# Sliding-window attention with scores made twice in 32-row tiles, so that probabilities come out transposed

## The chip, the cores and the metric

The kernel runs on one core of a Trainium2 chip. The time is that of one execution on the device, in microseconds, as the median of several; executions of one kernel mostly agree within about 1% here. Runs are compared only with runs of the kernel before that were taken on the same chip in the same rounds. In the views, PE is TensorE (PEld its weight loads, which overlap), DVE is VectorE, ACT is ScalarE, POOL is GpSimd. PEclk, the granted clock, is the share of full speed that the throttle let TensorE have. Tiles named `..._ps` take TensorE's results and lie in PSUM; one buffer of such tiles is called a bank here. A matmul shown as `32*128 32x128` uses 32 rows and 128 columns of the array and moves 128 columns through it; a tiling mode is the size of the part of the array that a matmul addresses.

## The reference

Two branches over the same `x` (2048 x 640, bfloat16) are mixed by a gate. The change concerns the first one, attention over a window of 256 keys with 32 heads of 20 columns:

```python
def _A_ref(x, wqkv, wo):                      # S = 2048, D = 640, H = 32, Dh = 20, W = 256
    q, k, v = ...                             # (x @ wqkv), split into heads
    scores = einsum('bhqd,bhkd->bhqk', q, k) * Dh ** (-0.5)
    mask = (idx[:, None] - idx[None, :] >= 0) & (idx[:, None] - idx[None, :] < W)
    p = softmax(where(mask, scores, -1e9))
    o = einsum('bhqk,bhkd->bhqd', p, v)
    return o.transpose(...).reshape(B, S, D) @ wo
# b = _B_ref(...): a recurrence over 64 segments of 32 with 8 memory rows, 32 heads of 192
g = sigmoid((x * gate_w).sum(-1, keepdims=True))
return g * _A_ref(x, ...) + (1 - g) * b
```

## The kernel before

Four parts run one after the other: the sliding branch (`branch_A`), projections for the tails of all segments (`tail_projections`), the recurrent branch (`branch_B`) and the mix. In the sliding branch a head has only 20 of the 128 rows that a full matmul contracts over (`128*128` in the views). Q and K of four heads share 128 rows, 32 each. To get one head's scores, Q is kept in four copies (`QTm`), each zero outside one head's rows; the matmul then runs over all 128 rows. The masks are added by two more matmuls, DVE finds the maximum, ACT takes the exponential, and PE transposes the probabilities for the product with V.

```python
# branch_A: P = 128, KT = 5 (640 / 128), NB = 16 query blocks, NG = 8 groups of 4 heads, NKB = 3 key blocks
ps_s = ctx.enter_context(tc.tile_pool(name="a_ps_s", bufs=5, space=bass.MemoryType.PSUM))
ps_t = ctx.enter_context(tc.tile_pool(name="a_ps_t", bufs=2, space=bass.MemoryType.PSUM))
ps_o = ctx.enter_context(tc.tile_pool(name="a_ps_o", bufs=1, space=bass.MemoryType.PSUM))
# [...] weights: Wq and Wk padded to 32 columns a head (WqP, WkP); m_first, m_last: 0 or -1e30
QTm = [[const.tile([P, NG, P], BF, name=f"QTm{b}_{r}") for r in range(4)] for b in range(2)]
for b in range(2):
    for r in range(4):
        (nc.vector if (b + r) % 2 == 0 else nc.gpsimd).memset(QTm[b][r][:], 0.0)
# [...] prep_units(qb) returns closures: load and transpose x, gate, and:
    def mk_qk(isq, g0):
        def u():
            xT = stt['xT']
            Wp = WqP if isq else WkP
            ng = min(4, NG - g0)
            pst = ps_s.tile([P, 512], FP32, name="qk_ps", tag="s")
            for gg in range(ng):
                g = g0 + gg
                for kt in range(KT):
                    nc.tensor.matmul(pst[:, gg * P:(gg + 1) * P],
                                     lhsT=Wp[:, kt, 4 * g:4 * g + 4, :].rearrange("p h d -> p (h d)"),
                                     rhs=xT[:, kt, :], start=(kt == 0), stop=(kt == KT - 1))
            src = pst[:, 0:ng * P].rearrange("p (g q) -> p g q", q=P)
            if isq:
                nc.scalar.mul(stt['QT'][:, g0:g0 + ng, :], src, scale)
                for r in range(4):
                    nc.gpsimd.tensor_copy(qms[qb][r][32 * r:32 * r + DH, g0:g0 + ng, :],
                                          stt['QT'][32 * r:32 * r + DH, g0:g0 + ng, :])
            else:
                nc.vector.tensor_copy(stt['KTb'][:, g0:g0 + ng, :], src)
                if g0 + ng >= NG:
                    kring[qb] = stt['KTb']
        return u
# [...] mk_v: V of the block, with a column of ones
# for each query block qb, with nxt = prep_units(qb + 1), qm = qms[qb], kbs = its 2 or 3 key blocks:
    def st_scores(h):
        g, r = h // 4, h % 4
        sp = ps_s.tile([P, 512], FP32, name="s_ps", tag="s")
        for ci, c in enumerate(kbs):
            need_mask = (c == qb) or (c == qb - (NKB - 1))
            nc.tensor.matmul(sp[:, ci * P:(ci + 1) * P], lhsT=qm[r][:, g, :], rhs=kring[c][:, g, :],
                             start=True, stop=not need_mask)
            if need_mask:
                nc.tensor.matmul(sp[:, ci * P:(ci + 1) * P], lhsT=ident[:],
                                 rhs=(m_last if c == qb else m_first)[:], start=False, stop=True)
        nmx = hp.tile([P, 1], FP32, name="a_nmx")
        nc.vector.tensor_reduce(out=nmx[:], in_=sp[:, 0:nk * P], axis=AX.X, op=ALU.max, negate=True)
        ex = hp.tile([P, NKB * P], BF, name="a_ex")
        nc.scalar.activation(out=ex[:, 0:nk * P], in_=sp[:, 0:nk * P], func=ACT.Exp, bias=nmx[:], scale=1.0)
        hs[h] = dict(ex=ex)

    def st_transpose(h):
        if h % 2 == 0:
            return
        pt_ps = ps_t.tile([P, 2, NKB, P], BF, name="pt_ps", tag="t")
        for a in range(2):
            ex = hs[h - 1 + a]['ex']
            for ci in range(nk):
                nc.tensor.transpose(pt_ps[:, a, ci, :], ex[:, ci * P:(ci + 1) * P], ident[:])
        pt = hp.tile([P, 2, NKB, P], BF, name="a_pt", bufs=4)
        if h % 4 == 1:
            nc.scalar.copy(pt[:, :, 0:nk, :], pt_ps[:, :, 0:nk, :])
        else:
            nc.vector.tensor_copy(pt[:, :, 0:nk, :], pt_ps[:, :, 0:nk, :])
        for a in range(2):
            hs[h - 1 + a]['pt'] = pt[:, a]

    def st_pv(h):
        pt = hs[h]['pt']
        half = h // HH
        if h % HH == 0:
            o_tiles[half] = ps_o.tile([P, HH, 32], FP32, name="o_ps", tag="o")
        ovh = o_tiles[half]
        for ci, c in enumerate(kbs):
            nc.tensor.matmul(ovh[:, h % HH, 0:DH + 1], lhsT=pt[:, ci, :], rhs=vring[c][:, h, :],
                             start=(ci == 0), stop=(ci == nk - 1))
        del hs[h]
        if h % HH == HH - 1:
            rl = op.tile([P, HH], FP32, name="rl")
            nc.vector.reciprocal(rl[:], ovh[:, :, DH:DH + 1].rearrange("p h o -> p (h o)"))
            nc.vector.tensor_tensor(out=an[:, half * HH:(half + 1) * HH, :], in0=ovh[:, :, 0:DH],
                                    in1=rl[:].unsqueeze(2).to_broadcast([P, HH, DH]), op=ALU.mult)
    nu = len(nxt)
    every = max(1, (HA - 4) // max(1, nu))
    ui = 0
    for i in range(HA + 6):
        if i < HA:
            st_scores(i)
        if 0 <= i - 3 < HA:
            st_transpose(i - 3)
        if 0 <= i - 5 < HA and i % 2 == 0:
            st_pv(i - 6)
            st_pv(i - 5)
        if ui < nu and i >= 2 and (i - 2) % every == 0:
            nxt[ui](); ui += 1
    while ui < nu:
        nxt[ui](); ui += 1
# [...] transposes of `an`, output projection (10 matmuls), gate, store
# the whole kernel
early, late, last = weights.resident[:34], weights.resident[34:-2], weights.resident[-2:]
# early: loaded while branch_A runs; late: issued after it, ahead of tail_projections; last: ahead of branch_B
branch_A(...); tail_projections(...); branch_B(...); mix_out(...)
```

## Time and profile before

| | us |
|---|---|
| time before, median of the first 3 runs | 2617.16 |
| sliding branch in the profiled run, up to the tail's first matmul | 526.9 |
| tail projections, up to the first recurrent matmul | 185.8 |
| recurrent branch and mix | 1887.3 |

The prediction below shows the stages, a block's groups and the waits. Two more views matter for what follows. The first is the head of the page of the kernel before: busy time by engine, then PE's busy share and the granted clock in 40 slices of the span, in tenths.

```profile
PE 2249.0 (86%) x49877; PEld 1664.5 (64%) x49893; DVE 1190.4 (46%) x3578; ACT 1115.8 (43%) x2433; POOL 601.9 (23%) x1782
...
PE   7888889889888888888898888889888888889885
...
PEclk9899998989999899999999999999998999999987
```

The second is 100 us in the middle of the sliding branch. The columns are stretch, length, busy time (and instructions) of PE, PEld, DVE, ACT and POOL, granted clock, DMA share, GB/s.

```profile
200.00:300.00 100.00, 88.41 (x1405) 74.51 (x1410) 72.94 (x161) 73.00 (x139) 22.16 (x50) 0.92 0.07 20
```

The sliding branch is the first eight slices. PE is busy for seven to nine tenths of each, and its clock there is about as high as elsewhere: 0.92 in this stretch. Busy time does not say at which clock it was spent, so the two lines are read together.

### The profile page before, as it was taken

The numbers are of one execution on the slowest core, as the hardware profiler recorded it, in microseconds if no ns is written. First come the engines' busy times: TensorE is split into PE (matmuls) and PEld (weight loads), VectorE is DVE, ScalarE is ACT, GpSimd is POOL, SyncE is SP. The second block draws the span as 40 slices with busy tenths as digits, with TensorE's granted clock in tenths as the row PEclk, the third lists the DMA queues.
The fourth block names the chain that finished last, engine by engine and source line by source line (L and its number), as shares of the span: only waits on it lengthen the run. The fifth ranks groups of instructions, "written<-read, shape, count | busy, mean of one in ns | idle before, by whom it ended". The sixth has DMA issues, their size and how long they took to land.

```text
span 2600.0 us, 113795 instructions
## 1 busy us (share of the span) xinstructions
PE 2249.0 (86%) x49877; PEld 1664.5 (64%) x49893; DVE 1190.4 (46%) x3578; ACT 1115.8 (43%) x2433; POOL 601.9 (23%) x1782
## 2 busy tenths in 40 slices
PE   7888889889888888888898888889888888889885
PEld 5777777679465666666666656666666566566663
DVE  5777777723233443444344334434443444334433
ACT  4777777712233333333333333333333333333333
POOL 7622222050122222222222222222222221222220
PEclk9899998989999899999999999999998999999987
DMA  6600000085588888888888888888888888888887
GB/s 211 204 17 17 17 17 15 9 253 154 143 273 264 268 284 278 281 278 291 289 274 282 290 268 271 290 287 283 281 282 272 279 270 271 280 285 278 286 274 235
DMA packets 299154, 591.76 MB, mean 228 GB/s; under 512 B 102552, under 2 KB 112032, under 8 KB 298656
## 3 DMA queue, kind: packets, MB, share of 16 engines
q1 hardware_dynamic: 275536, 525.43, 62.9%
q0 software_dynamic: 20160, 55.60, 6.5%
q8 instruction: 391, 6.41, 1.0%
q10 hardware_dynamic: 2960, 3.44, 0.4%
q14 instruction: 107, 0.88, 0.1%
HBM read 554.98 MB, written 36.97 MB: 228 GB/s over the span
## 4 chain that ended last, share of the span: by engine, by line
PE 52%; DMA 34%; ACT 10%; DVE 2%; issue 2%; SPq 0%; POOL 0%; ACTq 0%; DVEq 0%; POOLq 0%
DMA t_w<-w_packed 30%; PE ps_o L764 8%; PE ps_q L599 8%; PE ps_k L599 8%; PE ps_v L599 5%; ACT a_ex L195 4%; PE t_psum L440 3%; ACT a_pt L208 3%; PE qk_ps L124 3%; PE ps_pv L740 2%; PE tr_k L614 2%; PE S_ps L668 2%; PE t_psv L457 1%; PE pt_ps L205 1%; PE S_ps L661 1%
## 5 line engine op out<-in xcount | busy, mean ns | idle before, releaser
L599 PEld LDWEIGHTS <-t_hT 128*32 128x32 bf16 x15360 | 379.6, 98 | 302.5 <-issue 93.2
L764 PE MATMUL ps_o<-t_OT,w_o 128*128 128x40 bf16 x8960 | 333.2, 182 | 41.7 <-ACT t_OT L745 41.7
L764 PE MATMUL ps_o<-t_OT,t_w 128*128 128x40 bf16 x6400 | 269.5, 182 | 111.5 <-DMA t_w<-w_packed 99.9
L764 PEld LDWEIGHTS <-w_o 128*128 128x128 bf16 x8960 | 288.0, 98 | 49.0 <-issue 42.9
L764 PEld LDWEIGHTS <-t_w 128*128 128x128 bf16 x6400 | 209.6, 97 | 140.6 <-DMA t_w<-w_packed 136.7
L745 ACT CAST t_OT<-ps_pv 128x480 bf16<-128x480 f32 x256 | 143.2, 559 | 327.5 <-PE ps_pv L740 327.2
L195 ACT ACTIVATE a_ex<-s_ps,a_nmx 128x384 bf16<-128x384 f32 (+2 forms) x512 | 252.8, 576 | 65.9 <-DVE a_nmx L193 63.7
L646 POOL COPY t_K<-t_xqk 128x64 bf16<-128x64 bf16 x256 | 60.8, 237 | 936.5 <-PE S_ps L668 656.3
L193 DVE TENSOR_REDUCE a_nmx<-s_ps 128x1 f32<-128x384 f32 (+2 forms) x512 | 247.0, 524 | 33.7 <-PE s_ps L190 25.1
L604 ACT CAST t_tok<-ps_k 128x384 bf16<-128x384 f32 x256 | 122.7, 479 | 314.1 <-PE ps_k L599 314.1
L723 DVE TENSOR_TENSOR t_PTx<-PT_ps,mk_x 128x320 bf16<-128x320 f32 x256 | 125.2, 489 | 266.8 <-PE PT_ps L716 266.8
L599 PE MATMUL ps_q<-w_q,t_hT 128*32 128x384 bf16 x4096 | 225.9, 343 | 18.7 <-DVE t_hT L775 18.4
L599 PE MATMUL ps_v<-w_v,t_hT 128*32 128x384 bf16 x4352 | 230.1, 335 | 0.0
L599 PE MATMUL ps_k<-w_k,t_hT 128*32 128x384 bf16 x4096 | 222.4, 338 | 0.0
L637 DVE COPY t_K<-tr_k 128x256 bf16<-128x256 bf16 x256 | 74.0, 289 | 244.1 <-PE tr_k L614 242.8
L604 ACT CAST t_tok<-ps_q 128x384 bf16<-128x384 f32 x256 | 123.0, 481 | 129.7 <-PE ps_q L599 129.5
L187 PE MATMUL s_ps<-KT_blk,QTm 128*128 128x128 bf16 x1440 | 172.5, 225 | 4.5 <-ACT a_ex L195 4.0
L604 ACT CAST t_vtok<-ps_v 128x384 bf16<-128x384 f32 x256 | 122.7, 479 | 116.6 <-PE ps_v L599 115.2
L614 PEld LDWEIGHTS <-t_tok 128*128 128x128 bf16 x1536 | 87.6, 98 | 117.4 <-ACT t_tok L604 56.4
L775 DVE CAST t_hT<-ps_o 128x40 bf16<-128x40 f32 x63 | 12.6, 200 | 310.9 <-PE ps_o L764 310.9
L205 PE MATMUL pt_ps<-a_ident,a_ex 128*128 128x128 bf16 x1440 | 146.1, 221 | 8.8 <-ACT a_ex L195 1.5
L678 DVE TENSOR_REDUCE sm_mx<-S_ps 128x4 f32<-128x160 f32 x256 | 82.6, 323 | 145.6 <-PE S_ps L668 145.6
(138 smaller groups left out, 4608.1 us busy)
## 6 DMA issues: line engine op xcount, KB each, us to landing
t_w<-w_packed SPq DMA_DIRECT2D x704, 384.0 KB, 4.3
t_w<-w_packed SPq DMA_DIRECT2D x640, 320.0 KB, 4.2
xbqk<-t_qk SPq DMA_DIRECT2D x16, 768.0 KB, 5.4
t_xqk<-xbqk POOLq DMA_DIRECT2D x64, 192.0 KB, 4.7
w_v<-in_B_Wv_dram POOLq DMA_DIRECT2D x17, 384.0 KB, 8.2
w_q<-in_B_Wq_dram POOLq DMA_DIRECT2D x16, 384.0 KB, 4.9
w_k<-in_B_Wk_dram POOLq DMA_DIRECT2D x16, 384.0 KB, 5.5
xbv<-t_vt SPq DMA_DIRECT2D x64, 96.0 KB, 1.9
```

The lines of the kernel that those rows point to most:

```text
L124: nc.tensor.matmul(pst[:, gg * P:(gg + 1) * P], lhsT=Wp[:, kt, 4 * g:4 * g + 4, :].rearrange("p h d -> p (h d)"), rhs=xT[:, kt, :], start= ...
L187: nc.tensor.matmul(sp[:, ci * P:(ci + 1) * P], lhsT=qm[r][:, g, :], rhs=kring[c][:, g, :], start=True, stop=not need_mask)
L193: nc.vector.tensor_reduce(out=nmx[:], in_=sp[:, 0:nk * P], axis=AX.X, op=ALU.max, negate=True)
L195: nc.scalar.activation(out=ex[:, 0:nk * P], in_=sp[:, 0:nk * P], func=ACT.Exp, bias=nmx[:], scale=1.0)
L205: nc.tensor.transpose(pt_ps[:, a, ci, :], ex[:, ci * P:(ci + 1) * P], ident[:])
L599: nc.tensor.matmul(t[32 * j:32 * j + 32, 0:384], lhsT=tile_of(hT)[:, kt, :], rhs=w[:, j * 384:(j + 1) * 384], start=(kt == kts[0]), stop=( ...
L604: sc.op("ACT", act(384), lambda: nc.scalar.copy(tile_of(tok)[:], b["tile"][:, 0:384]), reads=[b], writes=[tok])
L614: nc.tensor.transpose(t[:, k, :], tok["tile"][:, k * P:(k + 1) * P], ident[:])
L678: nc.vector.tensor_reduce(out=x["mx"][:], in_=view(), axis=AX.X, op=ALU.max)
L723: nc.vector.tensor_tensor(out=tile_of(dst)[:], in0=PT["tile"][:, i, :, :].unsqueeze(2).to_broadcast([P, 2, 4, L]), in1=mk.unsqueeze(1).uns ...
L745: sc.op("ACT", act(480), lambda: nc.scalar.copy(tile_of(OT)[:].rearrange("p b j l -> p (b j l)"), o["tile"][:, 0:480]), reads=[o], writes= ...
L764: nc.tensor.matmul(t[:, dt * L:(dt + 1) * L], lhsT=w[:, r * D + dt * P:r * D + (dt + 1) * P], rhs=OT["tile"][:, b, i, :], start=(g == 0 an ...
```

## The change

The intent is to take the transposes and the masks off PE and the probability copies off DVE and ACT. The scores are made twice, each time in tiles of 32 rows, in the hope that these run beside one another in the array. The first set (queries on the output's partitions) serves only to find each row's maximum; a DVE instruction adds the mask and takes the maximum in one pass (556 ns for 384 columns in the trace after, and 83 ns for a second instruction that reads the maximum out). The negated maximum, and a second row with its rounding residue, become two more contraction rows of Q (K has +1 and -1 there). The second set (keys on the partitions) then gives scores less their maximum, transposed; ACT takes the exponential straight into the layout that the product with V needs, and POOL zeroes the masked corners. The probabilities of two to three key blocks wait in SBUF, so 18 weight tiles that were loaded during the sliding branch are now loaded after it. Code that was removed is shown above and left out here.

```diff
-        ps_s = ctx.enter_context(tc.tile_pool(name="a_ps_s", bufs=5, space=bass.MemoryType.PSUM))
+        ps_s = ctx.enter_context(tc.tile_pool(name="a_ps_s", bufs=2, space=bass.MemoryType.PSUM))
+        ps_m = ctx.enter_context(tc.tile_pool(name="a_ps_m", bufs=3, space=bass.MemoryType.PSUM))
 [...]
+        mask = const.tile([P, NKB * P], BF, name="a_mask")
+        nc.gpsimd.memset(mask[:], 0.0)
+        nc.gpsimd.affine_select(out=mask[:, 2 * P:], in_=mask[:, 2 * P:], compare_op=ALU.is_ge, fill=NEG, base=0,
                                 pattern=[[-1, P]], channel_multiplier=1)
-        nc.gpsimd.affine_select(out=m_first[:], in_=m_first[:], compare_op=ALU.is_gt, fill=NEG, base=0,
+        nc.gpsimd.affine_select(out=mask[:, 0:P], in_=mask[:, 0:P], compare_op=ALU.is_gt, fill=NEG, base=0,
                                 pattern=[[1, P]], channel_multiplier=-1)
 [...] ones2: +1 on row DH and -1 on row DH+1 of each 32 rows, 0 elsewhere; mts: zeroed, 2 of [P, 4, 4, 32]
-        QTm = [[const.tile([P, NG, P], BF, name=f"QTm{b}_{r}") for r in range(4)] for b in range(2)]
 [...] evacuation of Q and K:
+                        nc.scalar.mul(qt_[t][half][:], pst[:], scale)
+                    elif half:
+                        nc.vector.tensor_scalar(out=kt_[t][half][:], in0=pst[:], scalar1=ones2[:], scalar2=None, op0=ALU.add)
                     else:
-                        nc.vector.tensor_copy(stt['KTb'][:, g0:g0 + ng, :], src)
-                        if g0 + ng >= NG:
-                            kring[qb] = stt['KTb']
+                        nc.scalar.activation(out=kt_[t][half][:], in_=pst[:], func=ACT.Identity, bias=ones2[:], scale=1.0)
 [...] in place of st_scores, st_transpose and st_pv:
+        rows = lambda t, h: t[h // 16][32 * (h % 4):32 * (h % 4) + 32, (h // 4) % 4, :]
+        mx, pts, o_ps, an = {}, {}, {}, {}
+        def scores(t, h):
+            kbs = range(max(0, t - 2), t + 1)
+            sp = ps_s.tile([P, 512], FP32, name="s_ps", tag="s")
+            n = len(kbs) * P
+            def mm(i, c):
+                nc.tensor.matmul(sp[:, i * P:(i + 1) * P], lhsT=rows(qt_[t], h), rhs=rows(kt_[c], h), start=True, stop=True,
+                                 tile_position=(32 * (h % 4), 0))
+            def fin():
+                if h % HH == 0:
+                    mx[t, h // HH] = op.tile([P, HH], FP32, name="a_mx", tag="mx", bufs=3)
+                junk = op.tile([P, NKB * P], BF, name="a_junk")
+                nc.vector.tensor_tensor_reduce(out=junk[:, 0:n], in0=sp[:, 0:n], in1=mask[:, NKB * P - n:], op0=ALU.add, op1=ALU.max,
+                                               scale=1.0, scalar=-3.0e38, accum_out=mx[t, h // HH][:, h % HH:h % HH + 1])
+            return [lambda i=i, c=c: mm(i, c) for i, c in enumerate(kbs)], fin
+        def augment(t, half):
+            m = mx.pop((t, half))[:].rearrange("p (g r) -> p g r", r=4)
+            mt = mts[half]
+            nc.gpsimd.tensor_scalar(out=mt[:, :, :, DH], in0=m, scalar1=-1.0, scalar2=None, op0=ALU.mult)
+            nc.gpsimd.tensor_tensor(out=mt[:, :, :, DH + 1], in0=m, in1=mt[:, :, :, DH], op=ALU.add)
+            def pe():
+                ap = ps_m.tile([P, 4, P], FP32, name="aug_ps", tag="m")
+                nc.tensor.matmul(ap[:].rearrange("p g q -> p (g q)"), lhsT=ident[:], rhs=qt_[t][half][:].rearrange("p g q -> p (g q)"),
+                                 start=True, stop=False, skip_group_check=True)
+                for g in range(4):
+                    nc.tensor.matmul(ap[:, g, :], lhsT=mt[:, g].rearrange("p r d -> p (r d)"), rhs=ident[:], start=False, stop=(g == 3),
+                                     skip_group_check=True)
+                q = qap.tile([P, 4, P], BF, name=f"QA_{half}", tag=f"qa{half}")
+                nc.scalar.copy(q[:], ap[:])
+                qa_.setdefault(t, [None, None])[half] = q
+            return pe
+        def probs(c, h):
+            qbs = range(c, min(c + 3, NB))
+            n = len(qbs) * P
+            tp = ps_t.tile([P, 512], FP32, name="st_ps", tag="st")
+            def mm(i, q):
+                nc.tensor.matmul(tp[:, i * P:(i + 1) * P], lhsT=rows(kt_[c], h), rhs=rows(qa_[q], h), start=True, stop=True,
+                                 tile_position=(32 * (h % 4), 0))
+            def fin():
+                g, r = h // 4, h % 4
+                if r == 0:
+                    pts[c, g] = ptp.tile([P, 4, NKB * P], BF, name="a_pt")
+                pt = pts[c, g]
+                nc.scalar.activation(out=pt[:, r, 0:n], in_=tp[:, 0:n], func=ACT.Exp)
+                if r == 3:
+                    nc.gpsimd.affine_select(out=pt[:, :, 0:P], in_=pt[:, :, 0:P], compare_op=ALU.is_ge, fill=0.0, base=0,
+                                            pattern=[[0, 4], [1, P]], channel_multiplier=-1)
+                    if len(qbs) == 3:
+                        nc.gpsimd.affine_select(out=pt[:, :, 2 * P:], in_=pt[:, :, 2 * P:], compare_op=ALU.is_gt, fill=0.0, base=0,
+                                                pattern=[[0, 4], [-1, P]], channel_multiplier=1)
+            return [lambda i=i, q=q: mm(i, q) for i, q in enumerate(qbs)], fin
+        def values(t, g):
+            half = g // 4
+            if g % 4 == 0:
+                o_ps[half] = ps_o.tile([P, HH, 32], FP32, name="o_ps", tag="o")
+            if g == 0:
+                an[t] = op.tile([P, HA, DH], BF, name="an")
+            ov = o_ps[half]
+            kbs = range(max(0, t - 2), t + 1)
+            for h in range(4 * g, 4 * g + 4):
+                for c in kbs:
+                    nc.tensor.matmul(ov[:, h % HH, 0:DH + 1], lhsT=pts[c, g][:, h % 4, (t - c) * P:(t - c + 1) * P], rhs=v_[c][:, h, :],
+                                     start=(c == kbs[0]), stop=(c == kbs[-1]))
 [...] division by the sums; project(t): transposes of `an`, output projection, gate, store
+        LAG1, LAG2 = 22, 32
         for u in prep_units(0):
             u()
+        queue, aug = [], None
+        for n in range(HA * (NB + 2) + LAG2 + 1):
+            t, h = divmod(n, HA)
+            if h == 2 and t + 1 < NB:
+                queue += prep_units(t + 1)
+            if h == 0 and extra_units and 1 <= t < NB:
+                for _ in range(-(-len(extra_units) // (NB - t))):
+                    extra_units.pop(0)()
+            mms, fins = [], []
+            if t < NB:
+                a, f = scores(t, h)
+                mms.append(a)
+                fins.append(f)
+            c, hc = divmod(n - LAG1, HA)
+            if 2 <= c < NB + 2:
+                a, f = probs(c - 2, hc)
+                mms.append(a)
+                fins.append(f)
+            for i in range(3):
+                for a in mms:
+                    if i < len(a):
+                        a[i]()
+            for f in fins:
+                f()
+            if aug and h % HH == 2:
+                aug()
+                aug = None
+            if t < NB and h % HH == HH - 1:
+                aug = augment(t, h // HH)
+            q, hq = divmod(n - LAG2, HA)
+            if 2 <= q < NB + 2 and hq % 4 == 3:
+                values(q - 2, hq // 4)
+                if hq == HA - 1:
+                    queue += project(q - 2)
+            if queue and n % 2:
+                queue.pop(0)()
+        while queue:
+            queue.pop(0)()
 [...]
-    early, late, last = weights.resident[:34], weights.resident[34:-2], weights.resident[-2:]
+    early, late, last = weights.resident[:16], weights.resident[16:-2], weights.resident[-2:]
```

## The prediction

The forecast's sum: 2617 - 55 (sliding branch) + 11 (tail) = 2573, less 7 for a shorter maximum, 2566 us.

- The 7.1 us for scores in row tiles count two neighbours of different row groups as one slot. The trace before shows overlap only for 32-column tiles (16 starts in 0.66 us). The trace after shows it for row tiles (pairs within 10 ns).
- DVE's 0.65 us for a maximum rests on 556 ns for 384 columns. The trace before gives the same: its maxima of 256 and 384 columns take 414 and 549 ns, so 64 columns more are 67 ns.
- The 1024 "for 512 maxima" are DVE instructions, two for each maximum.
- Nothing was charged to DVE for what GpSimd does beside it; that it costs nothing was assumed.

In the paragraph on row tiles, the short matmul is the one at 1501.05 in the view below it, and the next is the one at 1501.18.

> **What bounds the kernel now.** I read the page's slices first, then the busy time by stretch of the span. The columns of the next view are: stretch, length, busy time (and instructions) of PE, PEld, DVE, ACT and POOL, granted clock, DMA share, GB/s.
>
> ```profile
> 26.40:524.00 497.60, 437.19 (x6991) 367.71 (x7008) 366.24 (x839) 368.34 (x731) 146.14 (x305) 0.94 0.18 56
> 528.00:715.00 187.00, 166.41 (x2253) 142.19 (x2253) 50.96 (x81) 43.29 (x80) 43.47 (x96) 0.95 0.65 186
> 715.00:2600.00 1885.00, 1630.14 (x40512) 1143.17 (x40504) 763.48 (x2639) 700.66 (x1616) 391.17 (x1341) 0.94 0.86 277
> ```
>
> The sliding branch is only the first 524 us; the tail projections (187 us) and the recurrent branch (1885 us) are not edited. So the change can move at most the first 498 us, plus the start of the tail stage through one line of the diff (where weights are loaded). In the sliding branch the chain of waits shows one block's output projection (32 heads) every 32.6 to 32.9 us. One block (233.07 to 265.69), by groups (busy, mean ns | idle before):
>
> ```profile
> L195 ACT ACTIVATE a_ex<-s_ps,a_nmx 128x384 bf16<-128x384 f32 x32 | 16.5, 596 | 4.5 <-DVE a_nmx L193 4.5
> L193 DVE TENSOR_REDUCE a_nmx<-s_ps 128x1 f32<-128x384 f32 x32 | 16.3, 549 | 2.0 <-PE s_ps L190 1.7
> L187 PE MATMUL s_ps<-KT_blk,QTm 128*128 128x128 bf16 x96 | 11.4, 226 | 0.0
> L205 PE MATMUL pt_ps<-a_ident,a_ex 128*128 128x128 bf16 x96 | 9.3, 220 | 0.5
> L208 ACT COPY a_pt<-pt_ps 128x768 bf16<-128x768 bf16 x8 | 6.5, 812 | 1.8 <-PE pt_ps L205 1.8
> L221 PE MATMUL o_ps<-V_blk,a_pt 128*128 128x21 bf16 x96 | 4.9, 174 | 1.1 <-ACT a_pt L208 0.8
> L210 DVE COPY a_pt<-pt_ps 128x768 bf16<-128x768 bf16 x8 | 4.4, 553 | 1.6 <-PE pt_ps L205 1.5
> ```
>
> A head costs DVE 549 + 553/4 ns and ACT 596 + 812/4 ns, but PE 11 matmuls: 3 scores, 2 masks, 3 transposes, 3 values. Busy overstates a pipelined engine, so I took the pitch from the timeline:
>
> ```profile
> 241.32 0.30 PE L221 MATMUL o_ps<-V_blk,a_pt 128*128 128x21 bf16 x6
> 241.48 0.22 PE L187 MATMUL s_ps<-KT_blk,QTm 128*128 128x128 bf16 x1
> 241.53 0.22 PE L190 MATMUL s_ps<-m_first,a_ident 128*128 128x128 bf16 x1
> ```
>
> Six value matmuls start in 0.16 us (27 ns each); a 128-column matmul starts every 55 ns. PE per block: 32 x (8 x 55 + 3 x 27 ns) = 16.7 us, and projections 8 us (80 of 55 ns, ten for V, ten for the output, transposes, gate): 24.7 us. The other 8 us of 32.65 are waits and a slow start: at each block's end the pipeline runs dry. Over 100 us PE waited:
>
> ```profile
> PE out_ps L255 <- ACT aT L250: 4.6, 4, 1.2
> PE o_ps L221 <- ACT a_pt L208: 2.5, 9, 0.3
> PE aT_ps L248 <- DVE an L227: 2.1, 4, 0.6
> ```
>
> and from 228 to 236 us the granted clock was 0.61, against 0.99 from 236 to 264. So PE bounds within a block, and latency at its seam.
>
> [...] No row tiles are in this trace; its 32-column tiles do overlap (16 matmuls of 384 columns start within 0.66 us, 41 ns each). [...] the second of these is a short matmul (its like start 40 ns apart), yet the next, in another mode, starts 130 ns after it; with its neighbours of the same kind a switch costs about 95 ns.
>
> ```profile
> 1501.05 0.20 PE L716 MATMUL PT_ps<-ident,b_Px 128*128 128x80 bf16 x1
> 1501.18 0.83 PE L599 MATMUL ps_q<-w_q,t_hT 128*32 128x384 bf16 x16
> ```
>
> [...] The build of the changed kernel has indeed 1024 for 512 maxima; no duration for the second is in this trace. [...]
>
> **The change part by part** (a steady block).
>
> PE. Removed: 64 masks, 96 transposes. Added: 96 scores by key in 32-row tiles, ten matmuls for the maxima (2 x 512 and 8 x 128 columns, 0.87 us). In the build order scores and probabilities stand partly alternated and always in different row groups: counting a neighbouring pair as one slot, 192 matmuls make 129 slots, x 55 = 7.1 us (10.6 us if nothing overlaps). Values 2.6, projections about 7.9, maxima 0.9, and 52 mode switches x 95 ns = 4.9. Sum **23.4 us** (26.9 without overlap), against 24.7.
>
> DVE. Removed: 8 copies (4.4 us), one K eviction (0.69), part of the gate and of the output scaling. A two-input DVE op of 320 columns from PSUM takes 489 ns (the recurrent branch)[...]; the accumulator read I put at 60 to 145 ns (a 128x1 op takes 145 ns alone, about 65 in a stream). About 0.65 us x 32 + 3.3 us of rest = **24 us**. This is the number that I know least.
>
> ACT. Removed 8 copies (6.5). Added two augmented-Q copies, a K eviction, a part of the output scaling (0.6 each). 32 x 0.5 (the pitch of exponentials in a run) + 5.5 = **21.5 us**. POOL: the 8 QTm copies of 609 ns go; 16 mask selections of 128x512 come. A 128x128 one takes 0.29 us and a 4-element one 0.19, so 512 take about 0.6: 10 us, plus 3 us: not a bound.
>
> Three engines at 21 to 24 us, coupled by two score banks and two probability banks (five before) and by PE's 20-matmul bursts (1.1 us): I add 10% and choose **26.5 us** a block for 32.65. The seam disappears, since blocks now run through in one pipeline.
>
> The pipeline is longer: key block c needs queries c to c+2, so values trail scores by 96 head steps. First score at about 28 us (26.4 before). Blocks 0 to 3 by DVE and PE: 18 + 21 + 24.5 + 25. Blocks 4 to 14: 11 x 26.5 = 291. The last block and the trailing 96 steps by ACT: 88 exponentials of 384 at 0.5, 32 each of 256 and 128 at 0.4 and 0.28, five sets of output copies: about 60 us. Sum 468 + 2 for the last output; it was 525 (the tail's first matmul stands at 526.9). **Gain 55 us** (plus or minus 11 for each us of block time).
>
> Tail. SBUF for the probabilities moves 18 weight tiles of 384 KB (7.1 MB; the 16 K tiles among them) from inside the sliding branch, where DMA was only partly used, to after it:
>
> ```profile
> 529.75 5.31 POOL L389 DMA_DIRECT2D w_v<-in_B_Wv_dram  x10 [56.42 <-DVE t_qk L447]
> ```
>
> Those loads started 3 us after the tail's first matmul and held DMA at a share of 1.0 from 535 to 570 us. The K tiles are needed by the 61st tail matmul, after 3.4 us; four tiles at about 1.05 us, issued at +3, land at about +9.5: 6 us of wait. The busy stretch grows by 18 us, in which PE before lost about a quarter: 5 us. **Cost 11 us.** Unedited: 1885 us.
>
> Net -44 us: 2617 - 44 = 2573. That a design with work moved so deliberately from DVE to ACT and POOL leaves the maximum nearer 0.6 than 0.65 us I find a little likelier than not (0.05 x 32 = 1.6 us a block if DVE bounds; I take half): **2566 us**.
>
> **The rivals.** (a) *PE bounds, no overlap of row tiles*: 26.9 us of PE and coupling make 29 to 30 a block; gain 15 to 30, tail lost: 2600 to 2615. For it: half of the tiles are not alternated, and 52 switches. Against: column tiles overlap here. (b) *DVE bounds*: a maximum with its read at 0.75 us is 27.3 us of DVE, 28.5 a block: 2595. (c) *ACT bounds and all else hides*: 22 to 23 a block, 2525 to 2535. For it: the longest single need is then 21.5; against: two banks each. (d) *The tail loses more*, 25 to 30 us, if K tiles come late for each group: 15 to 20 us on top of any of these.
>
> **Range and chances.** 24 us a block gives 2545, 28.5 gives 2595; with the tail's 8 to 20 and the fill, 8 in 10 lie within 2520 to 2610. The border of 2% is 2564.8, at my estimate: faster 0.49, same 0.47, slower 0.04 (it needs 36 us a block or a stall not seen).
>
> **What would show it.** Output projections of a steady block 26.5 us apart, without the clock of 0.61 at a seam; alternated row tiles starting some 28 to 35 ns apart; mode switches of about 95 ns; the maximum with its read at 0.6 to 0.7 us; DVE, PE and ACT each 80 to 90% busy there; the first tail matmul near 470 us; a wait of about 6 us on a K tile. It is wrong if row tiles don't overlap, if the accumulator read costs over 0.2 us, if POOL's selections take over 1 us, or if the tail stage passes 207 us.

## The result, and the profile after

The changed kernel is correct and slower: 2692.41 us (median of 4 runs, 2685.45 to 2697.68), against 2620.11 (median of 4, 2616.75 to 2627.81) for the kernel before. Ratios here and below are the mean time of one kernel's fast runs over that of the other's fast runs of the same rounds, so they are not quite the ratios of the medians. Here it is 1.027, with a 95% interval of 1.0233 to 1.0307.

The page's head and slices after:

```profile
PE 2322.3 (86%) x49074; PEld 1632.1 (61%) x49093; DVE 1125.0 (42%) x3894; ACT 1043.7 (39%) x2369; POOL 690.1 (26%) x1996
...
PE   6999999987978888888888888888888888888885
...
PEclk9666666668989989999999999999999989989997
```

PE's share is 86%, as before. Slices two to nine, most of the sliding branch, stand out in the last line: the clock there is 6 in place of 8 or 9, while PE's busy share is if anything higher. The stages, and the middle stretch, in the same columns as before:

```profile
26.40:578.00 551.60, 505.35 (x6251) 331.95 (x6268) 307.12 (x1167) 298.49 (x671) 228.48 (x496) 0.65 0.13 37
578.00:783.00 205.00, 168.60 (x2241) 144.81 (x2242) 50.70 (x80) 43.21 (x80) 52.50 (x113) 0.92 0.68 206
783.00:2696.00 1913.00, 1641.76 (x40533) 1150.07 (x40533) 762.32 (x2640) 700.15 (x1616) 389.65 (x1342) 0.94 0.85 274
```

```profile
200.00:300.00 100.00, 90.82 (x1203) 61.98 (x1205) 59.12 (x218) 56.24 (x125) 37.85 (x83) 0.65 0.05 14
```

DVE and ACT now do less than before in 100 us (59 for 73, 56 for 73), PE has fewer instructions (1203 for 1405) and yet more busy time. So the sliding branch is 51 us longer (578.1 for 526.9), the tail projections 19 us (205.0 for 185.8). The remaining 26 us between the two profiles are in the recurrent branch, which is not edited; in the other profiles that part lies anywhere from 1881 to 1922, and the profiled run of the kernel before, 2601.7, was faster than all the timed ones beside it. I do not count it: 51 and 19 make 70, and the medians differ by 72.

One block now takes 34.4 us. ACT's copies of the transposed output, one for each block, show it:

```profile
253.95 0.70 ACT L243 COPY aT<-aT_ps 128x640 bf16<-128x640 bf16 x1
288.29 0.70 ACT L243 COPY aT<-aT_ps 128x640 bf16<-128x640 bf16 x1
```

Is PE waiting? The largest group of PE's waits from 200 to 300 us (total us, times, longest one) says that it hardly is; all of PE's idle time there is 9 us, and no gap is over 0.5 us:

```profile
PE st_ps L197 <- ACT a_pt L205: 2.4, 9, 0.3
```

The groups from 300 to 500 us answer the durations that were predicted (busy, mean ns | idle before):

```profile
L197 PE MATMUL st_ps<-QA,KT 32*128 32x128 bf16 x558 | 66.6, 269 | 7.8 <-ACT a_pt L205 4.8 <-issue 2.8
L160 PE MATMUL s_ps<-KT,QT 32*128 32x128 bf16 x558 | 64.1, 269 | 0.0
L167 DVE CUSTOM_DVE_ANT_0 a_junk<-s_ps,a_mask 128x384 bf16<-128x384 f32 x186 | 98.9, 556 | 76.8 <-PE st_ps L197 38.4 <-PE s_ps L160 37.3
L205 ACT ACTIVATE a_pt<-st_ps 128x384 bf16<-128x384 f32 x186 | 84.7, 490 | 41.2 <-PE st_ps L197 34.8 <-PE s_ps L160 4.9
L167 DVE DVE_READ_ACCUMULATOR2_ANT a_mx<- 128x1 f32 x185 | 15.3, 83 | 0.0
L207 POOL TENSOR_SCALAR_AFFINE_SELECT a_pt<-a_pt 128x512 bf16<-128x512 bf16 x47 | 29.8, 634 | 75.3 <-ACT a_pt L205 75.3
```

DVE, ACT and POOL took what they were charged, and wait for PE. A score matmul has a mean of 269 ns, where 226 was seen before. A mean hides how this comes about; the trace's clock records hold only two values, 1.0 and 0.5, and stretches of 1.5 us show them (0.53 in one that a change falls into):

```profile
302.50:304.00 1.50, 1.20 (x20) 1.03 (x21) 1.04 (x4) 1.36 (x3) 0.63 (x1) 0.53 0.00 0
304.00:305.50 1.50, 1.17 (x29) 1.06 (x27) 0.31 (x1) 0.65 (x2) 0.00 (x0) 1.00 0.00 0
311.50:313.00 1.50, 1.28 (x32) 1.00 (x31) 1.50 (x7) 1.39 (x4) 1.04 (x2) 1.00 0.08 16
314.50:316.00 1.50, 1.38 (x21) 0.93 (x21) 0.98 (x5) 0.65 (x2) 0.84 (x3) 0.50 0.00 0
```

At 304 us, some 3 us after PE began the Q and K projections (20 matmuls over the whole array at a time), the clock goes to full; at 314, some 3 us after the larger of the two V projections, it is back at half. In this block it is full for about 10 of 34 us. The timeline shows the same kind of matmul on either side, first at full clock:

```profile
311.11 0.21 PE L160 MATMUL s_ps<-KT,QT 32*128 32x128 bf16 x1
311.11 0.21 PE L197 MATMUL st_ps<-QA,KT 32*128 32x128 bf16 x1
311.12 0.21 PE L160 MATMUL s_ps<-KT,QT 32*128 32x128 bf16 x1
311.13 0.21 PE L197 MATMUL st_ps<-QA,KT 32*128 32x128 bf16 x1
311.18 0.21 PE L160 MATMUL s_ps<-KT,QT 32*128 32x128 bf16 x1
...
311.33 0.39 PE L224 MATMUL o_ps<-V_blk,a_pt 128*128 128x21 bf16 x9
```

and at half clock:

```profile
287.08 0.31 PE L197 MATMUL st_ps<-QA,KT 32*128 32x128 bf16 x1
287.09 0.31 PE L160 MATMUL s_ps<-KT,QT 32*128 32x128 bf16 x1
287.19 0.31 PE L197 MATMUL st_ps<-QA,KT 32*128 32x128 bf16 x1
287.20 0.31 PE L160 MATMUL s_ps<-KT,QT 32*128 32x128 bf16 x1
```

At full clock two tiles of different rows start together, at times four (311.11 to 311.13), and the next follow 50 to 70 ns later; at half clock the pitch is 110 ns. The row tiles do overlap as hoped. What was given is a clock at which every slot costs twice as much.

The tail stage has its own lines. PE's longest waits from 560 to 800 us:

```profile
PE t_psum L484 <- DVE t_qk L491: 16.9, 1, 16.9
PE t_psum L484 <- DMA w_k<-in_B_Wk_dram: 1.6, 3, 1.0
```

and for the kernel before, from 500 to 720 us:

```profile
PE t_psum L440 <- DVE t_qk L447: 4.3, 1, 4.3
```

The weights came in time (1.6 us of wait for K tiles). DVE had to wait to copy a result into `t_qk`, because that buffer was still being written to memory (`xbqk`). After, and before:

```profile
DVE t_qk L491 <- DMA xbqk<-t_qk: 25.5, 1, 25.5
DVE t_qk L447 <- DMA xbqk<-t_qk: 14.3, 2, 12.8
```

The longest such write took 28.4 us from issue to landing, against 18.4 before, while weight loads kept the DMA at a share of 1.02 to 1.04 from 590 to 630 us (before: 1.00 to 1.04 from 535 to 565).

### The profile page after: what moved, and what is told of

Same layout as the page of the kernel before. It is cut to its first block, busy times and chain, and to the rows that moved or that the text cites. A ratio compares the mean times of both kernels' runs of the same rounds, so it can differ in the third digit from the quotient of the medians.

```text
span 2696.0 us, 112571 instructions
## 1 busy us (share of the span) xinstructions
PE 2322.3 (86%) x49074; PEld 1632.1 (61%) x49093; DVE 1125.0 (42%) x3894; ACT 1043.7 (39%) x2369; POOL 690.1 (26%) x1996
## 4 chain that ended last, share of the span: by engine, by line
PE 57%; DMA 35%; ACT 5%; issue 2%; DVE 1%; POOL 0%; SPq 0%; ACTq 0%; DVEq 0%; POOLq 0%
DMA t_w<-w_packed 31%; PE ps_q L643 8%; PE ps_o L808 8%; PE ps_k L643 8%; PE ps_v L643 5%; PE qk_ps L128 4%; PE st_ps L197 4%; PE t_psum L484 3%; PE s_ps L160 3%; PE ps_pv L784 2%; PE tr_k L658 2%; PE o_ps L224 2%; PE S_ps L712 2%; PE out_ps L250 1%; PE t_psv L501 1%
## 5 line engine op out<-in xcount | busy, mean ns | idle before, releaser
L167 DVE CUSTOM_DVE_ANT_0 a_junk<-s_ps,a_mask 128x384 bf16<-128x384 f32 (+2 forms) x512 | 260.3, 530 | 174.2 <-PE s_ps L160 91.7
L205 ACT ACTIVATE a_pt<-st_ps 128x384 bf16<-128x384 f32 (+2 forms) x512 | 223.5, 470 | 94.7 <-PE st_ps L197 76.8
L643 PE MATMUL ps_q<-w_q,t_hT 128*32 128x384 bf16 x4096 | 231.0, 349 | 18.7 <-DVE t_hT L819 18.4
L197 PE MATMUL st_ps<-QA,KT 32*128 32x128 bf16 x1440 | 184.8, 270 | 21.0 <-ACT a_pt L205 14.1
L160 PE MATMUL s_ps<-KT,QT 32*128 32x128 bf16 x1440 | 177.4, 268 | 2.0 <-DVE a_mx L167 1.3
L784 PE MATMUL ps_pv<-t_PTx,t_xv 128*64 128x160 bf16 x1536 | 143.1, 247 | 0.0
```

Source lines behind the costliest of these rows:

```text
L160: nc.tensor.matmul(sp[:, i * P:(i + 1) * P], lhsT=rows(qt_[t], h), rhs=rows(kt_[c], h), start=True, stop=True, tile_position=(32 * (h % 4) ...
L167: nc.vector.tensor_tensor_reduce(out=junk[:, 0:n], in0=sp[:, 0:n], in1=mask[:, NKB * P - n:], op0=ALU.add, op1=ALU.max, scale=1.0, scalar= ...
L197: nc.tensor.matmul(tp[:, i * P:(i + 1) * P], lhsT=rows(kt_[c], h), rhs=rows(qa_[q], h), start=True, stop=True, tile_position=(32 * (h % 4) ...
L205: nc.scalar.activation(out=pt[:, r, 0:n], in_=tp[:, 0:n], func=ACT.Exp)
L643: nc.tensor.matmul(t[32 * j:32 * j + 32, 0:384], lhsT=tile_of(hT)[:, kt, :], rhs=w[:, j * 384:(j + 1) * 384], start=(kt == kts[0]), stop=( ...
L784: nc.tensor.matmul(t[64 * a:64 * a + 64, 160 * b:160 * b + 160], lhsT=v[:, c:c + 64], rhs=p["tile"][:, a, :, :].rearrange("p j l -> p (j l ...
```

## The experiments

The theory after the result: the granted clock follows how much of the array is at work, and 32-row tiles, mostly two at a time, use too little of it; the block is slow because its PE work runs at half clock for most of the time. Its rivals: waits or the order of work make the block slow and the clock is a by-product; the two-set structure itself (double scores, lags, two score banks) is the cost; or the tail's loads are.

All ran in 3 rounds beside the kernel before, on one chip for each set: e1 to e4 together (before there 2622.03), e5 to e7 together (before 2608.59), e8 alone (before 2621.64).

### e1: the changed kernel with all 128 rows

```diff
-        rows = lambda t, h: t[h // 16][32 * (h % 4):32 * (h % 4) + 32, (h // 4) % 4, :]
+        rows = lambda t, h: t[h // 16][:, (h // 4) % 4, :]
-                                 tile_position=(32 * (h % 4), 0))     # in scores and in probs
```

This is wrong: each score sums four heads. Count and order of the instructions and every other engine's work stay. The changes of tiling mode go, so e1 alone does not separate them from the rows; e2 keeps them.

> The changed kernel, scores and probabilities on all 128 rows of the array instead of 32 (each score then sums four heads: wrong result on purpose, same instructions, same counts). Theory A (the granted clock falls because 32-row matmuls fill too little of the array): clock from 200 to 500 us goes from 0.65 to 0.9 or more, a block from 34.3 to about 27 us, total some 80 us under the changed kernel, about 2610. Rival B (the clock falls because PE keeps stopping at waits and two-deep buffers): clock stays near 0.65 to 0.7 and the total within 15 us of 2692. Rival C (row tiles are what makes the PE part cheap, clock or not): the pairs no longer overlap, 192 matmuls at 55 ns or more, slower than 2692.

Measured: 2583.8 us, ratio 0.9878 (0.9829 to 0.9927). The stretch from 200 to 300 us:

```profile
200.00:300.00 100.00, 93.61 (x1545) 81.09 (x1547) 74.36 (x279) 71.29 (x161) 50.51 (x111) 1.00 0.08 22
```

The clock is 1.00, a block takes 26.7 us and the tail's first matmul stands at 470.9: the branch is 107 us shorter than in the changed kernel, although no two score matmuls overlap any more (they start 55 ns apart). Neither the double scores nor the lags and the two banks make a block 34 us long. The row tiles do.

### e2: the changed kernel with 64 rows

```diff
-        rows = lambda t, h: t[h // 16][32 * (h % 4):32 * (h % 4) + 32, (h // 4) % 4, :]
+        rows = lambda t, h: t[h // 16][64 * (h % 4 // 2):64 * (h % 4 // 2) + 64, (h // 4) % 4, :]
-                                 tile_position=(32 * (h % 4), 0))
+                                 tile_position=(64 * (h % 4 // 2), 0))     # in scores and in probs
```

Also wrong (two heads are summed).

> As the first run but on 64 rows (two heads summed, wrong on purpose); mode switches and overlap of row groups stay, so it differs from the changed kernel in rows alone. Theory A: clock clearly above 0.65 (0.75 or more), total 30 to 80 us under 2692. Rival B (waits and mode switches hold the clock down): clock as before, total within 15 us of 2692. If it is as the changed kernel and the 128-row run is fast, the mode switches and not the rows are the cause.

Measured: 2668.02 us, ratio 1.0181 (1.0128 to 1.0235).

```profile
200.00:300.00 100.00, 93.42 (x1311) 65.37 (x1310) 63.09 (x234) 59.90 (x133) 41.30 (x90) 0.80 0.06 17
```

The clock lies between those of 32 and 128 rows, and so does the block, at 31.9 us. Changes of mode are all still there, at the same price as in the changed kernel (148 and 146 ns from a row tile's start to that of a full matmul, median at full clock), so the rows move the clock. The total is 24 us under the changed kernel's 2692, short of the 30 that were expected, and the two intervals just touch (1.0235 and 1.0233); what is read here is the trace.

### e3: the kernel before with 32-row scores

```diff
-                    nc.tensor.matmul(sp[:, ci * P:(ci + 1) * P], lhsT=qm[r][:, g, :], rhs=kring[c][:, g, :],
-                                     start=True, stop=not need_mask)
+                    nc.tensor.matmul(sp[:, ci * P:(ci + 1) * P], lhsT=qts[qb][32 * r:32 * r + 32, g, :],
+                                     rhs=kring[c][32 * r:32 * r + 32, g, :], start=(ci == 0), stop=(c not in edge),
+                                     tile_position=(32 * r, 0), skip_group_check=True)
# the mask matmuls follow the three scores
```

> The kernel before with only its scores by query put into 32-row tiles (masks, transposes and the rest as they were; correct result). Theory A: clock in the sliding branch falls from 0.94 to 0.7 to 0.85 since only 3 of 11 matmuls a head are small, and the branch gets slower by 10 to 60 us, although each score matmul is no dearer. Rival B: clock stays at 0.92 to 0.95; only the two mode switches a head cost, 2 x 95 ns x 512 = up to 97 us on PE if none is hidden, visible as gaps of 95 ns at full clock.

Measured: 2706.66 us, ratio 1.0329 (1.0283 to 1.0375), correct. From 200 to 300 us, and a pair of switches between 32-row and full matmuls:

```profile
200.00:300.00 100.00, 92.55 (x1266) 68.35 (x1267) 67.48 (x141) 66.29 (x125) 18.07 (x41) 0.90 0.05 13
```

```profile
312.88 0.34 PE L189 MATMUL s_ps<-KT_blk,QT_blk 32*128 32x128 bf16 x3
313.14 0.23 PE L194 MATMUL s_ps<-m_first,a_ident 128*128 128x128 bf16 x1
```

The block grows from 32.3 to 37.5 us, but the clock only falls from 0.92 to 0.90. The forecast of theory A, a clock of 0.7 to 0.85 and 10 to 60 us more, failed: the branch is 85 us longer (first tail matmul at 611.7). So here the clock is the smaller part: the order of work has a switch of tiling mode on both sides of every head's scores, 64 a block, and no tiles of other rows beside them. Three scores that start at 312.88 are followed by the mask at 313.14, 0.26 us later, where three slots of 55 ns would be 0.17. 64 x 95 ns are 6 us, about the 5.2 by which the block grew; this sum is an estimate, not a test. With transposes, masks and projections over the whole array around the scores, the clock is mostly kept. The last block but one shows how near that is to the edge: with the same work as those before it, it falls to half clock at 540 us, stays there for 37.5 us and takes 50.8 us:

```profile
541.00:577.00 36.00, 32.80 (x291) 23.10 (x291) 17.88 (x34) 17.04 (x31) 2.43 (x4) 0.50 0.01 2
```

The experiment does not separate the switches from the clock; it shows that row tiles can lose with little help from the clock.

### e4: the kernel before with 16 early weight tiles

```diff
-    early, late, last = weights.resident[:34], weights.resident[34:-2], weights.resident[-2:]
+    early, late, last = weights.resident[:16], weights.resident[16:-2], weights.resident[-2:]
```

> The kernel before with only the other part of the diff: 18 weight tiles loaded after the sliding branch rather than inside it. From the changed kernel's trace, where its tail stage is about 20 us longer: 15 to 25 us slower than before, all of it between 526 and 740 us as a longer wait on the staging of the tail projections. If the longer tail is due to something else: within 5 us of before.

Measured: 2642.24 us, ratio 1.0076 (1.0026 to 1.0126): 20 us in the medians, and in the traces the tail stage takes 203.0 us for 185.8. Of `t_psum`, the one wait on `t_qk`:

```profile
  PE t_psum L440: 17.2, 1
```

It is the same wait as that of 16.9 us in the changed kernel. The load shift costs 17 to 20 us by itself, with the attention left as it was.

### e5: the changed kernel with K in four masked copies

```diff
+        kms = [[const.tile([P, 4, 4, P], BF, name=f"a_km{b}_{i}") for i in range(2)] for b in range(5)]   # zeroed
+                    for r in range(4):
+                        nc.gpsimd.tensor_copy(kt_[t][half][32 * r:32 * r + DH + 2, r, :, :], ks[32 * r:32 * r + DH + 2, :, :])
-        rows = lambda t, h: t[h // 16][32 * (h % 4):32 * (h % 4) + 32, (h // 4) % 4, :]
+        qrows = lambda t, h: t[h // 16][:, (h // 4) % 4, :]
+        krows = lambda t, h: t[h // 16][:, h % 4, (h // 4) % 4, :]
-    early, late, last = weights.resident[:16], weights.resident[16:-2], weights.resident[-2:]
+    early, late, last = weights.resident[:8], weights.resident[8:-2], weights.resident[-2:]
```

This makes e1 correct: the trick of the kernel before (zeros outside one head's rows), here on K, with full-row matmuls and no tiling. It needs more SBUF, so only 8 weight tiles are loaded early.

> The changed kernel, made correct on 128 rows: K is kept in four copies that are zero outside one head's rows (8 GpSimd copies a block), so scores and probabilities contract over all 128 rows without tiles. The copies take SBUF, so 8 weight tiles instead of 16 load inside the sliding branch. Theory A (clock follows how much of the array is used): clock 0.98 or more from 200 to 400 us, a block 26.5 to 28 us as in the 128-row run, tail 8 to 10 us longer than there: about 2595, so 1% under the kernel before. If GpSimd's copies of K are late: block 30 us or more and waits of s_ps on POOL, total over 2620.

Measured: 2588.33 us (2583.1 to 2595.61), ratio 0.9928 (0.9876 to 0.9979), correct. It beats both kernels: 0.7% under the kernel before, and more under the changed one.

```profile
200.00:400.00 200.00, 187.42 (x3069) 163.84 (x3073) 143.25 (x536) 137.23 (x308) 132.07 (x274) 0.98 0.07 20
```

A steady block takes 26.7 us at a clock near 1 (27.2 in the mean of six). K is zero in all but 22 rows of each copy, and the clock is 0.98 all the same, for 0.65 in the changed kernel: here it goes with the number of rows addressed and not with how many of the weights are zero. Of the 107 us that the branch could gain, the first tail matmul at 485.8 keeps 92. The tail takes 209.0 us here, with a wait of 14.6 us for `t_qk` and one of 11.6 for a K tile.

### e6: only the scores by query over 128 rows

```diff
+        full = lambda t, h: t[h // 16][:, (h // 4) % 4, :]
-                nc.tensor.matmul(sp[...], lhsT=rows(qt_[t], h), rhs=rows(kt_[c], h), start=True, stop=True,
-                                 tile_position=(32 * (h % 4), 0))
+                nc.tensor.matmul(sp[...], lhsT=full(qt_[t], h), rhs=full(kt_[c], h), start=True, stop=True)
# and all of a head's scores before its probabilities, not alternated
```

> The changed kernel with only the scores by query on 128 rows and the probabilities on 32 (three of each in a row; wrong result on purpose), so that the tiling mode changes about twice as often as in the changed kernel while the array is used more. Theory A: clock 0.75 to 0.95, above the changed kernel's 0.65, in spite of more switches; blocks 32 to 36 us because of these. Rival B (mode switches and the waits they bring hold the clock down): clock at or under 0.65 and blocks over 37 us.

Measured: 2686.48 us, ratio 1.0208 (1.0109 to 1.0308). I had called this output wrong beforehand; it is correct, since the first set only shifts the softmax. The four runs fell into two groups, 2699.94 and 2696.77 (slow) and 2676.19 and 2647.76, and the profile is of a slow one, so nothing is read from its span, and its clock only as that of one slow run (slow means here: more than 1.5% above the kernel's fastest run):

```profile
200.00:300.00 100.00, 98.21 (x1079) 66.97 (x1078) 52.97 (x189) 50.48 (x106) 32.08 (x70) 0.70 0.04 11
```

PE is busy 98% of the time in this run, at a clock of 0.70, which lies between the forecasts of the two theories (0.75 or more; 0.65 or less). That a busy PE does not keep the clock up is shown by fast runs too: 91% at 0.65 in the changed kernel, 95% at 0.73 in e7. Half of the scores over all rows lifted the clock little here (0.73 and 0.83 in the next 200 us, with blocks that swing between 32.3 and 39.6 us). That more switches (two for each head) and the lost overlap ate what this gave is only argued; the time itself settles little.

### e7: projections spread over the block

```diff
-                queue += prep_units(t + 1)
+                u = prep_units(t + 1)
+                pr = (queue + [lambda: None] * 2)[:2]
+                queue = [u[0], u[1], pr[0], u[2], u[5], pr[1], u[3], u[6], u[7], u[4]] + queue[2:]
-            if queue and n % 2:
+            if queue and (n >= 32 * NB or h in (2, 3, 6, 11, 14, 17, 19, 22, 25, 27, 31)):
```

If the full-array projections are what lifts the clock, they should lift it more often when they do not all come together. The work is the same.

> The changed kernel (32-row tiles, correct) with the same work in another order: its four bursts of 20 full-array projections of Q and K are spread over a block, one every 8 heads, instead of four within 8 heads. In the changed kernel the clock goes to 1.0 about 3 us after the first of them and falls to 0.5 some 5 us after the last. Theory A with a memory of a few us: each burst keeps the clock up for 5 us or more, so the clock is 0.8 or more and the total 40 to 90 us under 2692. If one burst of 2 us is too short to lift the clock: 0.5 to 0.6 and a total of 2700 to 2760. Rival B (waits, not rows): clock and total as the changed kernel within 15 us.

Measured: 2668.77 us, ratio 1.0231 (1.0174 to 1.0287), correct.

```profile
200.00:300.00 100.00, 94.60 (x1244) 64.80 (x1245) 60.29 (x222) 57.73 (x127) 40.26 (x88) 0.73 0.06 17
```

From 0.65 the clock goes to 0.73 here (0.66 to 0.73 in the four stretches of 100 us), the block from 34.4 to 33.6 us. The direction is right, but the gain is small, short of the 0.8 and the 40 us that were forecast, and the ratio's interval overlaps the changed kernel's own (1.0233 to 1.0307): in time this one is inconclusive.

### e8: full-array matmuls that are thrown away

```diff
+            if h % 4 == 0:
+                for _ in range(3):
+                    nc.tensor.matmul(sp[:], lhsT=ident[:], rhs=WkP[:, 0, 0:16, :].rearrange("p h d -> p (h d)"),
+                                     start=True, stop=True)
```

> The changed kernel with work that is thrown away: ahead of the scores by query of every fourth head, three more matmuls over the whole array (128 rows, 128 columns out, 512 columns moving), whose result the real scores overwrite. The output stays correct. That is 24 such matmuls in a block of 32 heads[...]. Theory A (the granted clock follows how much of the array is at work, and short 32-row tiles use too little of it): the granted clock of the sliding branch rises from 0.65 to 0.85 or more, a block takes 30 to 32.5 us in place of 34.3 although it has more to do, and the whole is 10 to 40 us under the changed kernel's 2692. Rival B (the branch is slow through waits or the order of work, and the clock is a by-product or stays at 0.65): a block takes 39 to 44 us, the branch 80 to 150 us longer, and the whole lies at 2750 or above. In between (2690 to 2745): the clock rises by too little to pay for the added work, which leaves A as the direction only if the clock is read above 0.72.

Measured: 2702.84 us (2694.34 to 2708.32), ratio 1.0313 (1.0254 to 1.0373), correct. From 200 to 300 us:

```profile
200.00:300.00 100.00, 91.70 (x1241) 55.74 (x1254) 56.86 (x212) 54.60 (x122) 38.12 (x84) 0.85 0.06 16
```

Neither side's time came true; it fell in the stretch that I had left between, with the clock above the 0.72 that was to leave theory A as the direction. The clock rises from 0.65 to 0.85 (0.82 from 26.4 to 580 us). A block takes 34.5 us (output copies at 253.48 and 287.93), as without the added work. At an unchanged clock, 5.2 us more of work at full clock (24 matmuls of 512 columns, 216 ns each) would have made it 34.4 + 5.2 / 0.65 = 42 us. So useless full-array work paid for itself by lifting the clock, and gained nothing on top; the tail's first matmul is 14 us later (592.4) because the fill and the end of the branch got longer too. As a cure it fails; as a test it shows that adding array work, with nothing else removed, moves the clock. The interval of its ratio overlaps that of the changed kernel, so in time the two cannot be told apart.

### All of them side by side

The clock and PE's busy share are those of 200 to 300 us, the block is a mean over three to six blocks around there. The last column is my own estimate, worked out from the code and one measured duration: the columns that the block's matmuls move, each weighted by its share of the 128 rows, at 128 columns in 55 ns, over the block's time. For the changed kernel that is 192 score tiles x 128 x 1/4, 80 x 128 for Q and K, 3200 each for V and for the output, 1280 for transposes, 2048 for the maxima, 2016 for the values: 28,100 columns or 12.1 us of 34.4.

| kernel | block us | PE busy % | clock | array in use (estimate) |
|---|---|---|---|---|
| after | 34.4 | 91 | 0.65 | 35% |
| e7, spread | 33.6 | 95 | 0.73 | 36% |
| e6, half of the scores full (slow run) | 39.8 | 98 | 0.70 | 40% |
| e2, 64 rows | 31.9 | 93 | 0.80 | 46% |
| e8, added work | 34.5 | 92 | 0.85 | 50% |
| e3, before with row tiles | 37.5 | 93 | 0.90 | 50% |
| before | 32.3 | 88 | 0.92 | 70% |
| e5, masked K | 27.2 | 94 | 0.97 | 74% |
| e1, 128 rows | 26.7 | 94 | 1.00 | 75% |

The clock goes with the last column and not with PE's busy share; the kernel with the least busy PE of all, the one before, has a high clock. As a table this is an association over nine kernels, with two pairs that break the order (e6 and e7, and e8 and e3 at the same estimate).

The traces say more, step by step. In all ten sliding branches, every stretch at one clock lasts a multiple of 3.41 us. For each such step, from 100 us on to the tail, the columns of all matmuls that start in it were summed with the same weights, each by its share of the 128 rows; at full clock some 8,000 columns fit into a step (512 took 216 ns). After a step with under 2500 the next one was at half clock in 357 of 359 cases; after one with over 3500 it was at full clock in 664 of 664. A limit of 2970, fitted on the kernel before alone, tells the next step's clock right in 136 of 139 steps of the changed kernel and in 1132 of 1190 of all nine other traces. This holds whichever clock the step itself had, so a half clock, which halves the columns moved in a step (128 columns every 107 ns in place of 56), tends to keep itself: the slow block of e3 has 2302 to 3014 in its steps from 540 to 568 us. Columns without their weights do worse: with the best limit over all 1314 steps they miss 253, PE's busy share 447, the weighted columns 54. So the estimate of what the throttle follows is: columns moved times rows addressed, over 3.41 us, with a limit at about 37% of the whole array at full clock (2970 of some 8,000 columns). It is a fit to these traces and not a test: no run was planned to cross the limit and come back.

## Why the prediction was wrong

**The total.** Predicted 2566 us (2520 to 2610), measured 2692. Of the 126 us that are missing, about 108 are in the sliding branch (first tail matmul at 578.1, predicted near 470), 8 in the tail (19 for 11), 7 are the bonus that I granted to a shorter maximum, and 3 are the base, which was 2620 in these rounds.

**The step that failed** is the sum for PE: it charges 55 ns to each slot, a duration read at full clock, to get "Sum **23.4 us** (26.9 without overlap), against 24.7". As work the sum was about right: 34.4 us at a clock of 0.65 are 22.4 us of full-clock time. As time it was wrong: a slot took its 55 ns for only 10 of every 34 us and about 107 for the rest, because the clock was not a constant but an answer to the matmuls that the change removes (256 over the whole array a block: scores, masks and transposes) and puts in their place (192 over a quarter of it). "24 us a block gives 2545, 28.5 gives 2595" spans no block above 28.5; the note that a slower outcome "needs 36 us a block or a stall not seen" named the size of the surprise without its cause.

**The sign was in the prediction.** It shows a clock of 0.61 at the block's seam, against 0.99 within, and reads it as the seam's latency: "The seam disappears, since blocks now run through in one pipeline." In the changed kernel PE does run through (its longest waits are 2.4 us in 100), and the clock is 0.65 all the same. What the seam lacked was array work: in the step before the clock fell there, from 226.4 us on, the columns weighted by rows (see the table's section) were 2833, against 6712 in the step before that. The trace has two speeds (0.50 and 1.00) and steps of 3.41 us, and which of the two is granted did not follow busy time: PE had been busy at half clock for over 20 us, and the rise came some 3 us after the full-array projections began. The forecast charged nothing for the clock. Nor would a busier PE have been the cure: it was busy 91%.

**Step by step.** "Row tiles overlap": right, pairs start within 10 ns of each other at full clock, a pair every 56 ns in the median; e1 shows that the overlap was worth less than what it cost, 26.7 us without it at clock 1.00 against 34.4 with it. "Mode switches of about 95 ns": right at full clock (146 ns from a row tile to a full matmul in the median of 59, and 152 the other way in 16, where 55 pass without a change); at half clock it was about 135 (242 for 107). "The maximum with its read at 0.6 to 0.7 us": right, 556 + 83 = 639 ns; the 7 us taken off for a faster one were not there, and DVE was no bound. POOL's selections at "about 0.6": right, 634 ns. "DVE, PE and ACT each 80 to 90% busy there": wrong, PE 91, DVE 59, ACT 56, since two of them wait for a slow third. "Output projections of a steady block 26.5 us apart": wrong at 34.4, and right for the same instruction counts at full clock, 26.7 in e1, with the first tail matmul at 470.9. That match is partly luck: e1 has neither the overlap nor the 4.9 us of switches on which the 26.5 rested (its PE sum in the prediction's terms is 10.6 + 2.6 + 7.9 + 0.9 = 22.0). Two of the prediction's sums are also off, by too little to matter: its own figures for the exponentials of the end (88 x 0.5 + 32 x 0.4 + 32 x 0.28) give 65.8 us before any copies, not 60, and half of 1.6 us a block is worth 9 us at its 11 per us, not 7.

**The tail.** "6 us of wait" on K tiles was 1.6; the busy stretch cost more. What the sum lacked is the way out: results of the tail go to memory while the moved loads fill the DMA (a share of 1.02 to 1.04), and the longest such write took 28.4 us for 18.4, so the copy into `t_qk`, PE's banks and then PE stood still for 16.9 us (4.3 before). e4 isolates it: 17 us in the trace, 20 in the medians, where 11 were predicted. This is the term that was mis-sized; its direction was right.

**The rivals.** Three of the four rivals varied which engine bounds the block, each at its full-speed durations; none had the clock. The fourth (the tail) came out at 19 us, between the 11 of the sum and the 25 to 30 that it named.

**What stays open.** Whether the throttle counts just what the fit over the steps says; whether four row tiles at once (heads of the same group side by side), which happens here only now and then, would use enough of the array to hold the clock if it were the rule, which was not tried; and how much of e3's loss is switches.

## What to carry to other kernels

When a change replaces full-array matmuls by tiles of fewer rows, read the granted clock of a stage that already runs such tiles, or test one, before charging full-speed durations; a busy share near 90% said nothing of the clock here (91% at 0.65, 88% at 0.92). The trace of the kernel before already held the limit: sum the columns that each 3.41 us (the step in these traces) would move, weighted by rows, and compare with the steps after which the clock fell. If the operand has room, zeroing the other heads' rows and contracting over all 128 gave the same result here at nearly full clock (0.98 in e5), and was worth 7 us a block (27.2 for 34.4). When loads are moved to a stage, look also at the writes of that stage which go on beside them, and at the buffers that wait for these (16.9 us of PE here, for 4.3 before).
